# Gated linear attention feeding a cosine-gated MLP: token-major attention outputs turned on the tensor engine, and an order planned with new costs

## The chip, the cores and the metric

The kernel runs on one core of one Trainium2 chip. The metric is the device time of one execution in microseconds (us), as the median over several runs; lower is better. Names used below: PE is the tensor engine (PEld its weight loads), ACT the scalar engine, DVE the vector engine, POOL the GpSimd engine, SP the engine that only issues DMA here.

## The reference

Two stages follow each other. The first is a gated linear attention over 4 batches, 8 heads, 768 tokens and 48 channels; the second multiplies all 3072 tokens (384 features each) through an MLP with the gate h * cos(h):

```python
f = 1.0 / (1.0 + np.exp(-f_logit))
for t in range(S):
    state = f[:, :, t, :, None] * state + np.einsum('bhd,bhe->bhde', k[:, :, t], v[:, :, t])
    y[:, :, t] = np.einsum('bhd,bhde->bhe', q[:, :, t], state)
x = y.transpose(0, 2, 1, 3).reshape(B * S, H * D)      # 3072 x 384
h = x @ w_in                                           # 3072 x 2048
out = (h * np.cos(h)) @ w_out                          # 3072 x 384
```

## The kernel before

**Tiling.** The recurrence is cut into chunks of 128 tokens: 6 for each batch, 24 in all. Within a chunk the products of decays become a cumulative sum of logarithms, so that scaled q and k, one masked score matrix per head and one carried state per batch give the outputs by matmul. The MLP takes the finished chunks as units: four of 128 tokens, then ten of 256 (`UNITS`). Chunks go through the attention singly for the first four and in pairs after that (`GROUPS`).

**One chunk of attention**, with the lines of the listing:
- `chunk_load` (327) issues the DMAs of f, v, k and q, 192 KB each. Most go through SP. For chunk 0, k and q go through ACT; v of the first two chunks and q of the second go through POOL.
- `decay_group` (344) takes exp and log on ACT (352, 355), a cumulative sum on PE (367, 370), and two exponentials on ACT that give the scales b and bi (377).
- `attend` (385) scales q and k (395, 400, on POOL or DVE) and casts v to bf16 (404, POOL). The bf16 v goes into a buffer `vz` in which each head's 48 columns stand between zeros. Then q and k are turned so that channels lie on partitions: for chunks below `NPE` = 6 by twelve PE transposes and three evictions (421, 430, 432), for the others by one DMA transpose issued from SP (436). Scores are made by 8 matmuls (447) and masked on DVE (452). The new state takes 8 matmuls with 48 moving columns (466), then 475 and 479; it lies in `sz`, also between zeros.
- The outputs are made feature-major at once, which is the layout that the MLP reads as moving operand. For each of three blocks of 128 features, windows of `vz` (or `sz`) stand still and the masked scores (or turned q) move with 128 columns (506, 510). A window holds one head's columns at their place in the block and zeros around them. That gives 10 matmuls a chunk, and 6 more where there is a state. One copy (520 on ACT or 522 on DVE) brings the block to `xT`.

**One unit of the MLP** (`moe`, 526): groups of matmuls with w_in (540), each filling 512 columns of a PSUM bank; a Sin on ACT with a bias of pi/2 kept in a tile `halfpi` (547), which is the cosine; a product on DVE (551); then matmuls with w_out, 16 for each 128 tokens (561), a copy (570, 572) and the output DMA from SP (575).

**What sets the order.** Every operation is entered in a planner (`Plan`) with the engines that could run it and a cost in ns for each. `Plan.run` is a list scheduler: it takes the operation that could start first, gives it an engine and a buffer, and goes on. The kernel then issues exactly this order, so each engine runs a fixed list in sequence and waits on semaphores. A changed cost, buffer or dependence anywhere can therefore move instructions everywhere. Priorities only break ties. The weights come in eight DMAs from POOL (317), which the planner books on SP and which depend on chunk 0's v. PSUM has eight banks, shared by caps: scores 2, "mi" (sums, transposes, state, outputs) 4, MLP 5.

Of the kernel before, what the change touches and what calls it, by code (L numbers as in the profile page):

```python
# [9 lines left out]
F32 = mybir.dt.float32  # L10
BF16 = mybir.dt.bfloat16
AF = mybir.ActivationFunctionType
HALF_PI = math.pi / 2.0
# [78 lines left out]
class Op:  # L92
    __slots__ = ("seq", "eng", "fn", "prio", "table", "deps", "vals", "alloc", "start",
                 "end", "lat", "waiting", "after", "grp", "frees")


class Plan:


    SEM = 70.0  # L100

# [3 lines left out]
    def op(self, eng, fn, reads=(), writes=(), prio=0.0, table=None, lat=0.0, grp=None):  # L105
        o = Op()
        o.seq, o.fn, o.prio, o.table, o.lat, o.grp = len(self.ops), fn, prio, table, lat, grp
        o.eng, o.frees = eng, None
        o.deps, o.alloc, o.vals = set(), [], []
        for v in reads:  # L110
            o.deps.update(v.writers)
        for v in writes:
            w = getattr(v, "whole", v)
            if w.pool is not None:
                o.alloc.append(w)
            if v.writers:

                o.deps.add(v.writers[-1])
        for v in list(reads) + list(writes):
            v = getattr(v, "whole", v)  # L120
            if v.pool is not None and v not in o.vals:
                o.vals.append(v)
                v.uses += 1
        for v in writes:
            v.writers.append(o)
        o.after = []
        self.ops.append(o)
        return o
# [6 lines left out]
    def run(self):  # L135
        engs = ("PE", "ACT", "DVE", "POOL", "SP")
        free = dict.fromkeys(engs, 0.0)
        table, lock = "E", None
        left = {}
# [8 lines left out]
        n = len(self.ops)  # L148
        while len(order) < n:
            best = None  # L150
            for o in ready:
                at = max([d.end + (0.0 if e0 == d.eng == "PE" else self.SEM)
                          for d in o.deps for e0 in (next(iter(o.eng)),)], default=0.0)
                ok = True
                for v in o.alloc:
                    if v.slot is not None:
                        continue
                    b = v.pool.best()
                    if b is None:
                        ok = False  # L160
                        break
                    at = max(at, b[0] + self.SEM)
                if not ok:
                    continue
                pick = None
                for e, cost in o.eng.items():
                    if e == "ACT" and lock is not None and o.grp != lock and o.table is not None:
                        continue
                    s = max(at, free[e])
                    sw = 1300.0 if e == "ACT" and o.table not in (None, table) else 0.0  # L170
                    if pick is None or s + cost + sw < pick[0]:
                        pick = (s + cost + sw, s, e, cost)
                if pick is None:
                    continue
                key = (pick[1], o.prio, o.seq)
                if best is None or key < best[0]:
                    best = (key, pick[1], o, pick[2], pick[3])
# [16 lines left out]
            o.start, o.end = s, s + cost + o.lat  # L194
            free[e] = s + cost
            o.eng = e
# [20 lines left out]
def kernel(  # L217
# [23 lines left out]
    NPE = 6  # L241
# [31 lines left out]
    vS = slots("v", nld, [128, H, D], F32)  # L273
    spS = slots("sp", 5, [128, H, 64], zero=272.0)
# [3 lines left out]
    VW = D + 128  # L278
    vzS = slots("vz", 4, [128, H * VW + 128], zero=700.0)
    qktS = slots("qkt", 4, [128, 3 * NP, C])  # L280
    amS = slots("am", 4, [128, 4, C])
    SW = 128 + 2 * D + 128
    szS = slots("sz", 3, [128, NP, SW], zero=650.0)
# [26 lines left out]
    def load_weights(part, i, prio):  # L310
        if part == 0:
            dst = w_in_v[i]
            src = moe_w_in.rearrange("(km p) f -> p km f", p=128)[:, :, i * 512:(i + 1) * 512]
        else:
            dst = w_out_v[i]
            src = moe_w_out.rearrange("(kf p) m -> p kf m", p=128)[:, i * 4:(i + 1) * 4, :]
        o = P.op({"SP": 2000.0}, lambda e, dst=dst, src=src: nc.gpsimd.dma_start(
            out=dst.ap, in_=src), writes=[dst], prio=prio, lat=2500.0)
        o.deps.add(first_v[0])
# [5 lines left out]
    first_v = []  # L325

    def chunk_load(b, c, prio):
        vals = []
        for pool, src in ((fS, f_logit), (vS, v), (kS, k), (qS, q)):
            t = Val(pool)  # L330
            ap = src[b, :, c * C:(c + 1) * C, :].rearrange("h p d -> p h d")
            if prio < 1 and pool in (kS, qS):
                P.op({"ACT": 600.0}, lambda e, t=t, ap=ap: nc.scalar.dma_start(out=t.ap, in_=ap),
                     writes=[t], prio=prio, lat=3300.0)
            elif prio < 2 and pool in (vS, qS):
                o = P.op({"POOL": 1000.0}, lambda e, t=t, ap=ap: nc.gpsimd.dma_start(out=t.ap, in_=ap),
                         writes=[t], prio=prio, lat=3300.0)
            else:
                P.op({"SP": 1080.0}, lambda e, t=t, ap=ap: nc.sync.dma_start(out=t.ap, in_=ap),  # L339
                     writes=[t], prio=prio, lat=2200.0)  # L340
            vals.append(t)
        return vals
# [42 lines left out]
    def attend(b, c, ld, bt, bi, prio):  # L385
        _, vf, kf, qf = ld
        tok = b * S + c * C

        qk, vz = Val(qkS), Val(vzS)
# [9 lines left out]
        for par in range(2):  # L399
            P.op({"POOL": 550.0, "DVE": 350.0} if fast else {"POOL": 550.0}, lambda e, par=par: E(e).tensor_mul(  # L400
# [3 lines left out]
        o = P.op({"POOL": 510.0}, lambda e: nc.gpsimd.tensor_copy(  # L404
            out=vz.ap[:, 128:].rearrange("p (h w) -> p h w", w=VW)[:, :, 0:D], in_=vf.ap),
            reads=[vf], writes=[vz], prio=prio)
        first_v.append(o)
# [5 lines left out]
        if tok < NPE * C:  # L413
# [21 lines left out]
        else:  # L435
            P.op({"SP": 2000.0}, lambda e: nc.sync.dma_start_transpose(out=qkt.ap, in_=qk.ap),
                 reads=[qtd] + ktd, writes=[qdt] + kz, prio=prio, lat=2500.0)
# [22 lines left out]
        if c < NCH - 1:  # L460
            ps, S_out = Val(miS), Val(szS)

            def pes(e):
                o = ps.ap[:, 0:H * D].rearrange("p (h d) -> p h d", d=D)
                for h in range(H):
                    nc.tensor.matmul(o[:, h, :], lhsT=qk.ap[:, (NP + h) * C:(NP + h + 1) * C],  # L466
                                     rhs=vz.ap[:, 128 + h * VW:128 + h * VW + D],
                                     start=(h == 0), stop=(h == H - 1))
            P.op({"PE": 8 * 30.0}, pes, reads=ktd + [vz], writes=[ps], prio=prio, lat=170.0)
# [3 lines left out]
            else:  # L473
                st = Val(stS)
                P.op({"DVE": 530.0}, lambda e: nc.vector.tensor_add(  # L475
                    out=st.ap, in0=psv(), in1=S_in.ap[:, :, 128:128 + 2 * D]),
# [3 lines left out]
                out=S_out.ap[:, :, 128:128 + 2 * D], in0=srcap(),  # L480
# [5 lines left out]
        py = Val(miS)  # L486
        jobs = []
        for t in range(KM):
            for h in range(H):
                r = h * D - t * 128  # L490
                if -D < r < 128:
                    jobs.append((t, "a", h, r))
            if S_in is not None:
                for p in range(NP):
                    r = p * 2 * D - t * 128
                    if -2 * D < r < 128:
                        jobs.append((t, "s", p, r))

        def pey(e):
            o = py.ap.rearrange("p (a n) -> p a n", n=C)  # L500
            for i, (t, kind, n, r) in enumerate(jobs):
                first = all(j[0] != t for j in jobs[:i])
                fl = dict(start=(i == 0), stop=(i == len(jobs) - 1))
                if kind == "a":
                    w0 = 128 + n * VW - r
                    nc.tensor.matmul(o[:, t, :], lhsT=vz.ap[:, w0:w0 + 128],  # L506
                                     rhs=ams[n // 4].ap[:, n % 4, :], **fl)
                else:
                    w0 = 128 - r
                    nc.tensor.matmul(o[:, t, :], lhsT=S_in.ap[:, n, w0:w0 + 128],  # L510
                                     rhs=qdt.ap[:, n, :], **fl)
        rd = [vz, qdt] + ams + ([S_in] if S_in is not None else [])
        P.op({"PE": len(jobs) * N128}, pey, reads=rd, writes=[py], prio=prio, lat=170.0)
        x = xT[tok // C]

        def yev(e):
            d = x.ap
            s = py.ap[:, 0:KM * C].rearrange("p (a n) -> p a n", n=C)
            if e == "ACT":
                nc.scalar.copy(out=d, in_=s)  # L520
            else:
                nc.vector.tensor_copy(out=d, in_=s)
        P.op({"ACT": 380.0, "DVE": 530.0}, yev, reads=[py], writes=[x], prio=prio)


    def moe(t0, T):
# [6 lines left out]
        for j in range(KF // G):  # L533
            ph, co = Val(phS), Val(coS)

            def g1(e, j=j, ph=ph):
# [10 lines left out]
            P.op({"ACT": 640.0}, lambda e, ph=ph, co=co: nc.scalar.activation(  # L547
                out=co.ap, in_=ph.ap, func=AF.Sin, bias=halfpi),
# [6 lines left out]
        for i in range(T // 128):  # L555
# [12 lines left out]
            def ev(e, po=po, ot=ot):  # L568
# [7 lines left out]
                out=out[r0:r0 + 128, :], in_=ot.ap), reads=[ot], prio=pr, lat=2000.0)  # L576

    halfpi = cpool.tile([128, 1], F32, name="halfpi")
    nc.vector.memset(halfpi, HALF_PI)
# [59 lines left out]
```

## Time and profile before

| | before |
|---|---|
| median of 7 runs | 200.92 us (200.03 to 201.82) |
| the profiled execution: time, and span from first to last instruction | 201.82 us, 200.0 us |
| PE busy | 178.3 us, 1960 matmuls |
| ACT busy | 151.7 us |
| DVE busy | 143.0 us |
| POOL busy | 54.9 us |
| DMA | 34.15 MB, 171 GB/s over the span |

Busy time is the union of an engine's instructions. A matmul's row shows its latency, and matmuls overlap, so the pace of PE is read from the chain that ended last, where a run of n matmuls stands with the time it took. Idle time is put down to what released the engine. The granted PE clock is 1.00 over the whole core.

### The profile page before, as it was taken

What the parts mean: (1) busy time and instruction counts of PE and PEld (TensorE: products, weight loads), DVE (VectorE), ACT (ScalarE), POOL (GpSimd) and SP (SyncE); (2) the same over time, 40 slices, a digit from 0 to 9 for tenths busy, and PEclk for the clock granted to TensorE, in tenths of its full rate; (3) what the DMA queues carried; (4) which work ended last, traced back from release to release, by engine and by line L of the source; (5) the groups of instructions that cost most, each with busy time, mean ns of one, the idle gap of its engine ahead of it and who ended that gap; (6) DMA issues with size and microseconds to landing.
All of it is one profiled execution on the core that took longest, in us unless ns stands there. A gap on an engine that the chain in (4) does not pass through costs nothing.

```text
span 200.0 us, 5037 instructions
## 1 busy us (share of the span) xinstructions
PE 178.3 (89%) x1960; PEld 142.3 (71%) x1960; DVE 143.0 (71%) x248; ACT 151.7 (76%) x259; POOL 54.9 (27%) x86
## 2 busy tenths in 40 slices
PE   0359776989979999999999999999999999899992
PEld 0249765986868787787787887786887878678660
DVE  7865753775889889599689598598595998854500
ACT  4457746869999797798998799798796999727510
POOL 8775520412530230250301412711312316000000
PEclk9999999999999999999999999999999999999999
DMA  7999999999609989979999999898899855911012
GB/s 145 218 216 225 219 208 187 177 184 217 144 2 224 214 175 204 229 111 235 227 202 217 222 220 225 170 234 181 197 199 218 197 101 146 95 39 43 16 65 78
DMA packets 132328, 34.15 MB, mean 171 GB/s; under 512 B 125504, under 2 KB 132160, under 8 KB 132304
## 3 DMA queue, kind: packets, MB, share of 16 engines
q1 hardware_dynamic: 126320, 29.70, 72.5%
q0 software_dynamic: 3904, 3.74, 11.4%
q10 hardware_dynamic: 2080, 0.39, 1.0%
q8 instruction: 15, 0.25, 0.5%
q14 instruction: 9, 0.07, 0.1%
HBM read 25.17 MB, written 4.72 MB: 149 GB/s over the span
## 4 chain that ended last, share of the span: by engine, by line
PE 65%; DMA 15%; ACT 8%; issue 4%; DVE 3%; POOL 2%; SPq 2%; POOLq 0%; ACTq 0%; DVEq 0%
PE ps L561 25%; PE ps L540 24%; DMA qkt<-qk 7%; PE ps L506 5%; PE ps L447 5%; DMA w_out_bf<-in_moe_w_out_dram 4%; DMA v<-in_v_dram 4%; PE ps L510 2%; ACT b L377 2%; SPq L339 2%; PE ps L466 2%; PE ps L421 1%; ACT xT L520 1%; ACT bi L377 1%; ACT qkt L430 1%
## 5 line engine op out<-in xcount | busy, mean ns | idle before, releaser
L540 PE MATMUL ps<-xT,w_in_bf 128*128 128x256 bf16 (+1 forms) x672 | 70.1, 258 | 3.1 <-DMA w_in_bf<-in_moe_w_in_dram 1.6
L551 DVE TENSOR_TENSOR gT<-ps,cosh 128x512 bf16<-128x512 f32 x96 | 60.5, 683 | 15.4 <-ACT cosh L547 15.3
L561 PE MATMUL ps<-w_out_bf,gT 128*128 128x384 bf16 x384 | 70.1, 326 | 1.2 <-DMA w_out_bf<-in_moe_w_out_dram 1.1
L547 ACT ACTIVATE cosh<-ps,halfpi 128x512 bf16<-128x512 f32 x96 | 59.7, 694 | 8.3 <-PE ps L540 8.0
L540 PEld LDWEIGHTS <-w_in_bf 128*128 128x128 bf16 x672 | 57.4, 98 | 10.2 <-DMA w_in_bf<-in_moe_w_in_dram 1.8
L561 PEld LDWEIGHTS <-gT 128*128 128x128 bf16 x384 | 35.7, 98 | 20.7 <-issue 0.8
L452 DVE TENSOR_TENSOR am<-ps,umask 128x512 bf16<-128x512 f32 x48 | 30.9, 683 | 3.9 <-PE ps L447 3.2
L404 POOL CAST vz<-v 128x384 bf16<-128x384 f32 x24 | 12.8, 535 | 51.4 <-DMA v<-in_v_dram 30.2
L400 POOL TENSOR_TENSOR qk<-k,bi 128x192 bf16<-128x192 f32 x20 | 13.7, 686 | 36.0 <-ACT bi L377 27.0
L395 DVE TENSOR_TENSOR qk<-q,b 128x384 bf16<-128x384 f32 x21 | 12.6, 600 | 14.5 <-ACT b L377 14.5
L506 PE MATMUL ps<-am,vz 128*128 128x128 bf16 x240 | 22.3, 223 | 0.0
L479 POOL TENSOR_TENSOR sz<-st,b 128x384 bf16<-128x384 f32 x16 | 13.2, 825 | 27.0 <-DVE st L475 24.5
L570 ACT COPY ot<-ps 128x384 f32<-128x384 f32 x20 | 9.5, 475 | 14.2 <-PE ps L561 14.2
L447 PE MATMUL ps<-qkt 128*128 128x128 bf16 x192 | 16.3, 227 | 1.8 <-DMA qkt<-qk 1.2
L506 PEld LDWEIGHTS <-vz 128*128 128x128 bf16 x240 | 16.9, 100 | 1.4
L400 DVE TENSOR_TENSOR qk<-k,bi 128x192 bf16<-128x192 f32 x28 | 17.3, 631 | 0.0
L606 ACT ACT_TABLE_LOAD x12 | 15.4, 1283 | 2.2 <-issue 2.0
L510 PE MATMUL ps<-qkt,sz 128*128 128x128 bf16 x120 | 16.5, 219 | 0.0
L447 PEld LDWEIGHTS <-qkt 128*128 128x128 bf16 x192 | 12.9, 101 | 3.8 <-DMA qkt<-qk 2.0
L547 ACT ACT_TABLE_LOAD x12 | 15.4, 1283 | 0.2
L377 ACT ACTIVATE b<-ps 128x388 f32<-128x388 f32 x24 | 12.1, 503 | 3.7 <-PE ps L370 2.6
L367 PE MATMUL ps<-sp,umask 128*128 128x384 bf16 x24 | 8.0, 345 | 6.4 <-ACT sp L355 6.3
(38 smaller groups left out, 143.4 us busy)
## 6 DMA issues: line engine op xcount, KB each, us to landing
f<-in_f_logit_dram SPq DMA_DIRECT2D x24, 192.0 KB, 3.6
out_dram<-ot SPq DMA_DIRECT2D x24, 192.0 KB, 3.0
k<-in_k_dram SPq DMA_DIRECT2D x23, 192.0 KB, 4.2
v<-in_v_dram SPq DMA_DIRECT2D x22, 192.0 KB, 3.9
q<-in_q_dram SPq DMA_DIRECT2D x22, 192.0 KB, 3.8
w_in_bf<-in_moe_w_in_dram POOLq DMA_DIRECT2D x4, 384.0 KB, 5.8
w_out_bf<-in_moe_w_out_dram POOLq DMA_DIRECT2D x4, 384.0 KB, 7.8
v<-in_v_dram POOLq DMA_DIRECT2D x2, 192.0 KB, 6.2
```

The costliest lines, as they stand in the source:

```text
L377: nc.scalar.activation(out=o.ap, in_=pc.ap[:, 0:n], func=AF.Exp, scale=s)
L400: P.op({"POOL": 550.0, "DVE": 350.0} if fast else {"POOL": 550.0}, lambda e, par=par: E(e).tensor_mul(out=ktd[par].ap, in0=kf.ap[:, par:H: ...
L447: nc.tensor.matmul(o[:, i, :], lhsT=kz[g].ap[:, i, :], rhs=qdt.ap[:, h // 2, :], start=(i == 0), stop=(i == 3))
L452: nc.vector.tensor_mul(out=am.ap, in0=pa.ap.rearrange("p (a n) -> p a n", n=C), in1=umask[:, None, :].broadcast_to([128, 4, C]))
L479: P.op(cost, lambda e: E(e).tensor_mul(out=S_out.ap[:, :, 128:128 + 2 * D], in0=srcap(), in1=bt.ap[:, H * D:, None].broadcast_to([128, NP, ...
L506: nc.tensor.matmul(o[:, t, :], lhsT=vz.ap[:, w0:w0 + 128], rhs=ams[n // 4].ap[:, n % 4, :], **fl)
L510: nc.tensor.matmul(o[:, t, :], lhsT=S_in.ap[:, n, w0:w0 + 128], rhs=qdt.ap[:, n, :], **fl)
L540: nc.tensor.matmul(ph.ap[:, g * T:(g + 1) * T], lhsT=w_in_bf[:, m, f0:f0 + 128], rhs=x[:, m, :], start=(g == 0 and m == 0), stop=(g == G - ...
L547: P.op({"ACT": 640.0}, lambda e, ph=ph, co=co: nc.scalar.activation(out=co.ap, in_=ph.ap, func=AF.Sin, bias=halfpi), reads=[ph], writes=[c ...
L551: P.op({"DVE": 650.0}, lambda e, ph=ph, co=co, gv=gv: nc.vector.tensor_mul(out=gv.ap, in0=ph.ap.rearrange("p (g t) -> p g t", t=T), in1=co ...
L561: nc.tensor.matmul(po.ap[:, 0:d_model], lhsT=gT.ap[:, j, i * 128:(i + 1) * 128], rhs=w_out_bf[:, j, :], start=(j == 0), stop=(j == KF - 1))
L606: nc.scalar.preload_act_table_set("natural_log_exp_and_others")
```

## The change

Five things change.

1. The outputs of a chunk are made token-major. The masked scores of each head stand still, and v moves with 48 columns (8 matmuls); turned q stands still and the state of two heads moves with 96 columns (4 matmuls). So `vz` becomes a packed `vb`, `sz` loses its zeros, and their clearing goes. A copy brings the block to a bf16 tile `y`, three PE transposes turn it, and a second copy brings it to `xT`. (`NPX` is 24, so the branch that would turn it by DMA is never taken.)
2. `NPE` is 8 instead of 6: q and k are turned on PE for the first eight chunks, and by DMA from the ninth.
3. The Sin's bias is a constant in the instruction instead of the tile `halfpi`.
4. The weight DMAs are booked on POOL. Those of w_out depend on the k product of chunks 1 to 4 in turn, those of w_in on that of chunk 0. v and q of chunk 1 are loaded through SP, and chunk 0's k product is bound to POOL.
5. The planner gets a model of the two DMA rings and other costs for DMAs and for the Sin.

```diff
-    NPE = 6
+    GATES = [1, 2, 3, 4]
+    NPE, NPX, EVERY = 8, 24, 1
...
+                    if o.dma and e == "SP":
+                        s = max(s, ring[0] - self.RING)
...
-        o = P.op({"SP": 2000.0}, lambda e, dst=dst, src=src: nc.gpsimd.dma_start(
-            out=dst.ap, in_=src), writes=[dst], prio=prio, lat=2500.0)
-        o.deps.add(first_v[0])
+        o = P.op({"POOL": 850.0}, lambda e, dst=dst, src=src: nc.gpsimd.dma_start(
+            out=dst.ap, in_=src), writes=[dst], prio=prio, lat=2200.0, dma=2400.0 if part == 0 else 2200.0)
+        gate(o, 0 if part == 0 else GATES[i])
...
-            elif prio < 2 and pool in (vS, qS):
-                o = P.op({"POOL": 1000.0}, ...
+            elif prio < 1 and pool is vS:
+                eng, dma = {"POOL": 850.0}, nc.gpsimd
...
-            P.op({"POOL": 550.0, "DVE": 350.0} if fast else {"POOL": 550.0}, ...
+            o = P.op({"POOL": 550.0, "DVE": 350.0} if fast and tok else {"POOL": 550.0}, ...
...
-                    w0 = 128 + n * VW - r
-                    nc.tensor.matmul(o[:, t, :], lhsT=vz.ap[:, w0:w0 + 128],
-                                     rhs=ams[n // 4].ap[:, n % 4, :], **fl)
-                else:
-                    w0 = 128 - r
-                    nc.tensor.matmul(o[:, t, :], lhsT=S_in.ap[:, n, w0:w0 + 128],
-                                     rhs=qdt.ap[:, n, :], **fl)
+            for h in range(H):
+                nc.tensor.matmul(o[:, h, :], lhsT=ams[h // 4].ap[:, h % 4, :], rhs=vf.ap[:, h, :],
+                                 start=(h == 0), stop=(S_in is None and h == H - 1))
+            for p in range(NP if S_in is not None else 0):
+                nc.tensor.matmul(py.ap[:, p * 2 * D:(p + 1) * 2 * D], lhsT=qdt.ap[:, p, :],
+                                 rhs=S_in.ap[:, p, :], start=False, stop=(p == NP - 1))
...
-        P.op({"ACT": 380.0, "DVE": 530.0}, yev, reads=[py], writes=[x], prio=prio)
+        P.op({"ACT": 380.0, "DVE": 530.0}, copy(lambda: yt.ap, lambda: py.ap[:, 0:H * D]),
+             reads=[py], writes=[yt], prio=prio)
+                for t in range(KM):
+                    nc.tensor.transpose(out=pxv()[:, t, :], in_=yt.ap[:, t * C:(t + 1) * C],
+                                        identity=ident)
+            P.op({"PE": KM * N128}, tx, reads=[yt], writes=[px], prio=prio, lat=170.0)
+            P.op({"ACT": 380.0, "DVE": 330.0}, copy(lambda: x.ap, pxv), reads=[px], writes=[x],
+                 prio=prio)
...
-            P.op({"ACT": 640.0}, lambda e, ph=ph, co=co: nc.scalar.activation(
-                out=co.ap, in_=ph.ap, func=AF.Sin, bias=halfpi),
+            P.op({"ACT": 570.0}, lambda e, ph=ph, co=co: nc.scalar.activation(
+                out=co.ap, in_=ph.ap, func=AF.Sin, bias=HALF_PI),
```

## The prediction

> **What bounds the kernel now.** I read the page's busy times first, then four stretches of the span, then what PE waited for, then the chain of work that ended last for the pace of the matmuls, and the groups for durations.
>
> ```profile
> PE 178.3 (89%) x1960; PEld 142.3 (71%) x1960; DVE 143.0 (71%) x248; ACT 151.7 (76%) x259; POOL 54.9 (27%) x86
> ```
>
> PE leads, but 89% hides different stages. In the stretches the columns are length, then busy time of PE, PEld, DVE, ACT and POOL, the granted clock, the DMA share and GB/s:
>
> ```profile
> 0.00:18.30 18.30, 7.74 (x82) 6.73 (x83) 12.47 (x22) 9.32 (x18) 13.10 (x25) 1.00 1.12 199
> 18.30:60.00 41.70, 35.96 (x490) 29.91 (x489) 29.14 (x53) 32.89 (x53) 14.24 (x22) 1.00 0.93 169
> 60.00:170.00 110.00, 108.92 (x1183) 87.18 (x1181) 89.09 (x157) 96.36 (x168) 27.60 (x40) 1.00 0.94 198
> 170.00:200.00 30.00, 25.69 (x213) 18.46 (x210) 12.26 (x20) 13.12 (x23) 0.00 (x0) 1.00 0.26 56
> ```
>
> From 60 to 170 us PE is busy for 108.92 of 110 us, so there every microsecond taken off PE's list can come off the time. ACT (96.36, 88%) and DVE (81%) have some room, but not much. At the start PE waits: the first w_in matmul runs at 18.3 us. What PE waited for, in total, times, longest:
>
> ```profile
> PE ps L367 <- ACT sp L355: 6.3, 2, 5.4
> PE ps L421 <- POOL qk L395: 2.4, 1, 2.4
> PE ps L421 <- DVE qk L395: 2.0, 1, 2.0
> PE ps L540 <- DMA w_in_bf<-in_moe_w_in_dram: 1.6, 1, 1.6
> PE ps L447 <- DMA qkt<-qk: 1.2, 3, 0.5
> PE ps L561 <- DMA w_out_bf<-in_moe_w_out_dram: 1.1, 2, 0.6
> PE ps L540 <- ACT xT L520: 0.9, 2, 0.6
> ```
>
> The chain, as start, length and piece, gives the pace of each kind of matmul once they are back to back:
>
> ```profile
> 61.23 0.20 PE ps L466 x8
> 61.43 1.97 PE ps L540 x18
> 63.39 0.45 PE ps L447 x8
> 64.50 1.30 PE ps L561 x8
> 66.02 0.56 PE ps L506 x10
> ```
>
> That is 0.025 us for one with 48 moving columns, 0.056 with 128, 0.109 with 256, 0.163 with 384. Multiplied by the counts of the whole program (24 cumulative sums, 72 transposes, 192 scores, 160 state, 360 outputs, 192 + 480 with w_in, 384 with w_out) PE's list comes to 170.9 us. So some 29 us of the 200.0 us span are waiting: most of the first 18 us, 5.7 us up to 60 us, and about 4 us behind the last matmul.
>
> **Part by part: the outputs on PE.** Removed: 240 + 120 matmuls of lines 506 and 510 at 0.056 = 20.2 us. Added: 8 x 24 = 192 with 48 columns at 0.025 (the row of line 466, the same shape) = 4.8 us; 4 x 20 = 80 with 96 columns, which no row has: between 48 columns (0.025) and 128 (0.056) both ends give 2.0 and 4.5 us, and the line through 128 and 256 gives 0.043, so 3.4 us; 72 transposes at 0.056 (as line 447's 128 columns) = 4.0 us. Together 12.2, a saving of 7.9 us. Two more chunks with q and k turned on PE add 24 x 0.056 = 1.3 us. Net -6.6 us (164.3 us of PE work).
>
> Here a rule speaks against the change. The Trainium skill, "TensorE: Matmul & The Clock Gate", section "Back-to-back issue gap", says that in a stream of weight load and matmul pairs both set the spacing, about 81 ns at 128 columns. Each added matmul has its own 128-column weight load. If loads paced them at 0.081, the new outputs would cost (192 + 80 + 72) x 0.081 = 27.9 us against 360 x 0.081 = 29.2 before, and with the two chunks of transposes nothing would be left. The rows above decide: eight line-466 matmuls, each with its own load, took 0.20 us. I take the row, and keep the rule for the range.
>
> **The copies and ACT.** Counting the two built programs: ACT gets 16 y copies (0.479 each, the xT row) = +7.7, one xT copy less, 5 qkt copies less (0.586) = -2.9, 6 ot copies less = -2.9. DVE gets 8 y copies (0.557) = +4.5, 11 qkt (0.414) = +4.6, 6 ot (0.548) = +3.3, 10 k products less (0.631) = -6.3, a q product less = -0.6, six clearings less (3 x 0.698, 3 x 0.645) = -4.0, and xT copies that now read bf16: 12 at about 0.35 (estimate from qkt's 0.414 for 512) against 11 at 0.557 = -1.9. DVE: -0.6 us.
>
> The Sin loses its bias tile. The nearest row is the ACT copy of the same 128x512 size without one:
>
> ```profile
> L547 ACT ACTIVATE cosh<-ps,halfpi 128x512 bf16<-128x512 f32 x96 | 59.7, 694 | 8.3 <-PE ps L540 8.0
> L430 ACT COPY qkt<-ps 128x512 bf16<-128x512 bf16 x10 | 5.7, 591 | 6.7 <-PE ps L421 6.7
> ```
>
> The difference is 103 ns, but the operation and input type differ too. Bounds are nothing (all of it the operation) and 103 ns: 0 to -9.9 us. I take -9, near the row. ACT in sum: -7.6 us, or +1.4 if the bias is worth nothing. So neither ACT nor DVE gains load while PE sheds 6.6 us; POOL gets ten k products (0.686) and one q product (1.1), loses a clearing (1.4) and two loads' issue (1.9): +4.7 on 55 us, idle cover. Table loads stay 12 + 12.
>
> **The new wait.** Behind the outputs, a chunk now goes copy, PE, copy before the w_in matmuls can read it, where it was one copy. PE stands at the transposes until y is there: about 0.75 us behind the last output matmul (drain near 0.2, copy 0.48 to 0.56). In PE's new list, priced with the paces above, the work between the two is 0.7 to 1.8 us in 22 of 24 chunks; chunk 0 has 0.2 us, chunk 3 none. Queued behind the waiting transposes is the next w_out or w_in work. Cost: 0.75 for chunk 3, 0.5 for chunk 0, some hundredths for others: +1.5 us. Lower bound 0; upper bound under rivals. A further PSUM bank (px, within mi's four) can hold up sums; no PE wait on an eviction of mi stands in the list above beyond 0.7 us, so 0 to +2, taken +1 with other lateness of a new order.
>
> **The start.** Chunk 1's q product sat on POOL behind chunk 2's v cast, which waited for its load, and PE waited 2.4 us for it (line 395). In the new list it is on DVE right behind chunk 0's masks, about 1 us earlier; chunk 0's k product costs +0.6 us, both halves on POOL. The w_in issues of POOL stood at 9.2, 12.5, 14.9 and 18.7 us between waits; now the four stand together behind chunk 0's k product (about 10 to 13 us), so the 1.6 us wait for w_in should go. w_out pieces, at 20 to 36 us, now follow chunks 1 to 4: the 1.1 us goes too. Against it, DMA is full there (share 1.12), so what comes sooner pushes chunk 3's and 4's loads back; POOL's v cast of chunk 1 stands behind 3.2 us of issues; and w_out's DMAs wait for k products on POOL, with later v casts queued behind. Bounds -5 and +2; taken -2.5. SP issues as many DMAs as before (133), two of them loads instead of transposes.
>
> **The sum.** -6.6 (PE) + 1.5 (hop) + 1.0 (order) - 2.5 (start) = -6.6 us. The profiled execution took 201.82 us, span 200.0 and 1.8 around it, the slowest of the seven and 0.9 above the median; its span becomes 193.4. From the median: 200.9 - 6.6 = 194.3 us.
>
> **Rivals.**
>
> *DMA becomes the pace.* The DMA share is 0.94 from 60 to 170 us, at 198 GB/s, and POOL's v casts waited 30 us for loads. Two transposes less save 0.79 of 34.15 MB. Up to 170 us some 32.4 MB went, 191 GB/s; at that rate the loads end 4.1 us sooner, not 6.6 and more, and the start gives nothing: 197 us, and with part of the hop 198 to 200. Against it: slice 12 of the page moves only 2 GB/s, so the rings were not full all the time. Chance 0.18.
>
> *Slower: the hop is exposed.* Place: the three transposes per chunk, when the y copy is queued on ACT or DVE behind a Sin (0.69) or product that runs late. The gains (6.6 + 2.5) over 24 chunks are 0.38 us: from that mean exposure on the change loses. One Sin for each chunk is 16.6 us: 200.9 - 9.1 + 16.6 = 208 us; half of it is about no change. For it: ACT's list is dense (88%) and the copies' lists are fixed. Against it: ACT waited 8.0 us for line 510, so copies were ahead of PE, and PE waited for xT only 1.3 us. Chance 0.13 for slower, 202 to 208.
>
> *More gain.* The start gives its full 5 us and no hop shows: 190 us. Chance 0.04. That the change does not do what it says has little room: the counts are in the built program. Only the load-paced rule would void it, at about 200 us; it is within the 0.18.
>
> **How the numbers follow.** Forecast, 190.5 to 198: 0.65. A measurement of this kernel can tell about 0.5% (1.0 us) from no change. Faster by more: 0.65 + 0.04 + 0.14 of the DMA case = 0.83; within: 0.04; slower: 0.13. The range from 190.5 to 200.5 leaves out the slower case and the top gain.
>
> **What would show it.** Right: output matmuls of 48 columns at 0.025 and 96 near 0.043 in the chain; a Sin of 0.59 to 0.60; ACT's total near 144 and DVE's near 142 us; first w_in matmul near 16.5 us and no wait for w_in; PE busy about as full from 60 to 165 us; waits of PE for y copies about 1.5 us. Wrong: PE waits on y or xT copies above 9 us in sum, or PE idle behind loads or q/k DMA transposes in the middle, or a run of eight short matmuls above 0.4 us.

## The result, and the profile after

The changed kernel takes 198.59 us in the median of 13 runs (196.13 to 204.24); the kernel before takes 200.97 in 34 runs on the same chip. The ratio is 0.9831, with an interval of 0.9801 to 0.9861: 1.7% or 3.4 us faster, about half of the 6.6 us that were forecast. The ratio leaves out the executions that took over 1.5% more than the fastest of their kernel, none of the 34 before and 6 of the 13 after, the profiled one among them; the medians of all differ by 2.4 us.

The profiled execution took 199.56 us, with a span of 197.8. Its busy times on the page:

```profile
PE 175.8 (89%) x1968; PEld 137.1 (69%) x1968; DVE 141.4 (71%) x256; ACT 145.9 (74%) x263; POOL 58.7 (30%) x94
```

PE is busy for 2.5 us less, at the same 89%. ACT went down by 5.8 us and DVE by 1.6, POOL up by 3.8. The stretches, with the same columns as before (length, PE, PEld, DVE, ACT, POOL, clock, DMA share, GB/s):

```profile
0.00:18.30 18.30, 9.16 (x95) 7.60 (x96) 10.22 (x21) 8.89 (x17) 11.52 (x25) 1.00 1.10 182
18.30:60.00 41.70, 35.59 (x493) 28.79 (x492) 31.09 (x62) 31.61 (x53) 13.02 (x22) 0.96 1.07 192
60.00:170.00 110.00, 106.68 (x1201) 83.92 (x1199) 90.71 (x160) 94.97 (x176) 34.13 (x50) 1.00 0.94 188
170.00:198.00 28.00, 24.41 (x187) 16.75 (x185) 9.38 (x15) 10.41 (x20) 0.00 (x0) 1.00 0.13 50
```

PE's idle time, length less busy time, was 10.6, 5.7, 1.1 and 4.3 us in the four stretches; it is now 9.1, 6.1, 3.3 and about 3.4 (span less 170, less 24.4). The first stretch gained 1.4 us, the middle lost 2.2. And the second stretch has a clock of 0.96. In two pieces of it:

```profile
30.00:40.00 10.00, 6.82 (x73) 4.20 (x70) 7.10 (x14) 7.38 (x12) 3.05 (x5) 0.94 1.08 193
40.00:50.00 10.00, 8.79 (x119) 6.94 (x118) 6.63 (x14) 7.10 (x12) 4.36 (x8) 0.89 1.03 181
```

If the clock is either full or half, 0.94 and 0.89 mean 1.2 and 2.2 us at half clock, which stretches PE's work there by 1.7 us. What PE waited for (total, times, longest):

```profile
PE ps L391 <- ACT sp L379: 5.1, 1, 5.1
PE ps L583 <- DMA w_out_bf<-in_moe_w_out_dram: 3.2, 3, 1.4
PE ps L447 <- DVE qk L419: 2.1, 2, 1.6
PE ps L473 <- DMA qkt<-qk: 2.0, 1, 2.0
PE ps L447 <- POOL qk L424: 1.6, 2, 1.3
PE ps L538 <- DVE y L527: 1.0, 1, 1.0
...
PE ps L562 <- DMA w_in_bf<-in_moe_w_in_dram: 0.4, 1, 0.4
```

Line numbers have moved: L583 is w_out, L562 w_in, L447 the transposes of q and k, L473 the scores, L538 the new transposes of y. The wait for w_in is nearly gone (it was 1.6 us). The new hop, PE waiting for the copy of y before it can turn it, shows with 1.0 us, once. But w_out is now waited for 3.2 us, where it was 1.1, and one q/k DMA transpose for 2.0. The chain of work that ended last (start, length, piece) shows both, and the pace of the new matmuls:

```profile
32.22 6.55 DMA w_out_bf<-in_moe_w_out_dram
38.82 2.72 PE ps L583 x8
...
44.33 6.39 DMA w_out_bf<-in_moe_w_out_dram
...
53.53 0.20 PE ps L517 x8
53.73 0.17 PE ps L520 x4
...
54.82 0.17 PE ps L538 x3
...
93.39 7.67 DMA qkt<-qk
```

Eight output matmuls with 48 columns take 0.20 us, four with 96 take 0.17 (0.043 each), three transposes 0.17: the prices of the forecast. Eight w_out matmuls took 1.30 us before and 2.72 at 38.82 us: that is half clock. Two short waits stand right before them, one for y and one for this weight (in brackets the idle time before, and what ended it):

```profile
37.06 0.34 PE L538 MATMUL ps<-ident,y 128*128 128x128 bf16 x3 [1.02 <-DVE y L527]
38.82 2.72 PE L583 MATMUL ps<-w_out_bf,gT 128*128 128x384 bf16 x8 [1.42 <-DMA w_out_bf<-in_moe_w_out_dram]
```

The timeline shows why the weight came so late. First SP's own issues (start, length), then POOL's list:

```profile
12.50 6.93 SPq L363 DMA_DIRECT2D k<-in_k_dram  x1
19.48 5.47 SPq L363 DMA_DIRECT2D q<-in_q_dram  x1
```
```profile
28.96 0.50 POOL L429 CAST vb<-v 128x384 bf16<-128x384 f32 x1 [6.64 <-DMA v<-in_v_dram]
...
32.22 0.81 POOL L336 DMA_DIRECT2D w_out_bf<-in_moe_w_out_dram  x1
```

While the four w_in DMAs and the first w_out DMAs are under way, SP needs 6.93 and 5.47 us to issue two loads of chunk 3. In this execution the v of the same chunk, issued at 11.47, lets POOL's cast start only at 28.96. POOL waits 6.64 us for it, and behind it in POOL's list stands the third w_out issue.

Last, the Sin without its bias tile, as a group (total, mean ns, idle before):

```profile
L569 ACT ACTIVATE cosh<-ps 128x512 bf16<-128x512 f32 x96 | 53.4, 604 | 8.1 <-PE ps L562 4.8 <-DVE am L478 1.1
```

### The profile page after: what moved, and what is told of

The parts are those of the page before. It is cut to its first block, busy times and chain, and to the rows that moved or that the text cites. A ratio compares the mean times of both kernels' runs of the same rounds, so it can differ in the third digit from the quotient of the medians.

```text
span 197.8 us, 5063 instructions
## 1 busy us (share of the span) xinstructions
PE 175.8 (89%) x1968; PEld 137.1 (69%) x1968; DVE 141.4 (71%) x256; ACT 145.9 (74%) x263; POOL 58.7 (30%) x94
## 4 chain that ended last, share of the span: by engine, by line
PE 56%; DMA 21%; SPq 7%; POOL 6%; DVE 4%; issue 3%; ACT 1%; POOLq 0%; DVEq 0%; ACTq 0%
PE ps L583 24%; PE ps L562 22%; DMA w_out_bf<-in_moe_w_out_dram 13%; DMA qkt<-qk 4%; SPq L363 4%; SPq L462 3%; PE ps L473 3%; DMA q<-in_q_dram 2%; DMA v<-in_v_dram 2%; DVE am L478 2%; POOL w_in_bf L336 2%; POOL qk L424 1%; PE ps L391 1%; PE ps L517 1%; PE ps L520 1%
## 5 line engine op out<-in xcount | busy, mean ns | idle before, releaser
L583 PE MATMUL ps<-w_out_bf,gT 128*128 128x384 bf16 x384 | 72.4, 330 | 3.4 <-DMA w_out_bf<-in_moe_w_out_dram 3.2
L562 PE MATMUL ps<-xT,w_in_bf 128*128 128x256 bf16 (+1 forms) x672 | 70.3, 260 | 0.8 <-DMA w_in_bf<-in_moe_w_in_dram 0.4
L562 PEld LDWEIGHTS <-w_in_bf 128*128 128x128 bf16 x672 | 58.3, 99 | 8.3 <-issue 1.1
L569 ACT ACTIVATE cosh<-ps 128x512 bf16<-128x512 f32 x96 | 53.4, 604 | 8.1 <-PE ps L562 4.8
L583 PEld LDWEIGHTS <-gT 128*128 128x128 bf16 x384 | 35.6, 98 | 22.8 <-issue 4.3
L424 POOL TENSOR_TENSOR qk<-k,bi 128x192 bf16<-128x192 f32 x30 | 19.6, 664 | 23.3 <-ACT bi L401 14.9
L429 POOL CAST vb<-v 128x384 bf16<-128x384 f32 x24 | 12.9, 539 | 35.9 <-DMA v<-in_v_dram 21.7
L419 DVE TENSOR_TENSOR qk<-q,b 128x384 bf16<-128x384 f32 x20 | 13.1, 653 | 13.8 <-ACT b L401 10.6
L473 PE MATMUL ps<-qkt 128*128 128x128 bf16 x192 | 16.7, 227 | 2.1 <-DMA qkt<-qk 2.0
L592 ACT COPY ot<-ps 128x384 f32<-128x384 f32 x14 | 6.7, 479 | 13.3 <-PE ps L583 13.3
L473 PEld LDWEIGHTS <-qkt 128*128 128x128 bf16 x192 | 12.5, 101 | 3.4 <-DMA qkt<-qk 2.3
L527 ACT CAST y<-ps 128x384 bf16<-128x384 f32 x16 | 7.7, 480 | 8.4 <-PE ps L517 4.5
L447 PE MATMUL ps<-ident,qk 128*128 128x128 bf16 x96 | 9.7, 242 | 4.2 <-DVE qk L419 2.1
L376 ACT ACTIVATE f<-f 128x384 f32<-128x384 f32 x24 | 11.6, 517 | 1.1 <-DMA f<-in_f_logit_dram 1.0
L401 ACT ACTIVATE bi<-ps 128x384 f32<-128x384 f32 x24 | 12.0, 500 | 0.0
```

Of the source, the lines that this page charges most:

```text
L401: nc.scalar.activation(out=o.ap, in_=pc.ap[:, 0:n], func=AF.Exp, scale=s)
L419: P.op({"POOL": 1000.0, "DVE": 560.0} if fast else {"POOL": 1000.0}, lambda e: E(e).tensor_mul(out=qtd.ap, in0=qf.ap, in1=bt.ap[:, 0:H * D ...
L424: o = P.op({"POOL": 550.0, "DVE": 350.0} if fast and tok else {"POOL": 550.0}, lambda e, par=par: E(e).tensor_mul(out=ktd[par].ap, in0=kf. ...
L429: P.op({"POOL": 510.0}, lambda e: nc.gpsimd.tensor_copy(out=vf.ap, in_=v32.ap), reads=[v32], writes=[vf], prio=prio)
L473: nc.tensor.matmul(o[:, i, :], lhsT=kz[g].ap[:, i, :], rhs=qdt.ap[:, h // 2, :], start=(i == 0), stop=(i == 3))
L562: nc.tensor.matmul(ph.ap[:, g * T:(g + 1) * T], lhsT=w_in_bf[:, m, f0:f0 + 128], rhs=x[:, m, :], start=(g == 0 and m == 0), stop=(g == G - ...
```

## Experiments

The change bundles the outputs, the bias and a new plan. The theory was that the outputs on PE make the gain, and that the plan's start and the DMA queues take some of it back. The rivals: the bias or the plan alone make it, or the copies on ACT and DVE take the rest. A ratio is always to the kernel before on the same chip, with its 95% interval.

**e1: the bias alone.** The kernel before, all lists as they were:

```diff
-                out=co.ap, in_=ph.ap, func=AF.Sin, bias=halfpi),
+                out=co.ap, in_=ph.ap, func=AF.Sin, bias=HALF_PI),
```

> The kernel before with one edit: the Sin takes pi/2 as a constant instead of the tile halfpi; the planned cost stays, so every engine's list is unchanged. Theory (PE sets the time, ACT has room): Sin rows of about 0.60 instead of 0.69 us, ACT busy about 143 us, time 200 to 201 us, no more than 0.7 us better. Rival (the lighter Sin is what made the changed kernel faster): about 198 us.

0.9997 (0.9969 to 1.0025). The group in the profile of this run:

```profile
L547 ACT ACTIVATE cosh<-ps 128x512 bf16<-128x512 f32 x96 | 53.5, 601 | 13.4 <-PE ps L540 11.5
```

The Sin is 93 ns shorter (694 before), ACT has 6.2 us less work, and its idle time before the Sin grew from 8.3 to 13.4 us. Nothing is gained: ACT waited for PE.

**e2: the outputs alone.** Part 1 of the change in the kernel before, planned anew; bias tile, `NPE` = 6, DMA order and costs as before:

```diff
-                    nc.tensor.matmul(o[:, t, :], lhsT=vz.ap[:, w0:w0 + 128],
-                                     rhs=ams[n // 4].ap[:, n % 4, :], **fl)
+                nc.tensor.matmul(o[:, h, :], lhsT=ams[h // 4].ap[:, h % 4, :], rhs=vf.ap[:, h, :],
```

> The kernel before with the token-major outputs alone: packed v, 8 + 4 short matmuls, y copy, three PE transposes, second copy; NPE 6, the Sin's tile and the old planner and DMA costs stay. Theory (PE's saving is real and PE sets the time): PE's list falls by 20.2 - 12.2 = 7.9 us, some of it returned at the hop; 194 to 197 us. Rival (the copies and the hop eat it, and the gain of the changed kernel comes from the new planning and the Sin): 200 us or more.

1.0003 (0.9973 to 1.0032): nothing gained, and my expectation failed. Two stretches:

```profile
18.30:60.00 41.70, 32.69 (x456) 25.91 (x453) 29.38 (x55) 29.15 (x49) 12.13 (x19) 1.00 1.00 177
60.00:170.00 110.00, 106.10 (x1178) 82.68 (x1179) 94.28 (x164) 99.75 (x173) 29.94 (x44) 1.00 0.97 195
```

PE's busy time fell by 6.0 us (172.3), and its idle time rose from 21.7 to 27.5: 3.3 us more between 18 and 60 us (9.0 against 5.7) and 2.8 more in the middle (3.9 against 1.1). The saving is real, and this order can't use it.

**e3: third and fourth w_out early.** The changed kernel, with these two DMAs moved to directly behind the second in POOL's list; no other list changes:

```diff
+    for o in w_out_ops[2:]:
+        order.remove(o)
+    i = order.index(w_out_ops[1]) + 1
+    order[i:i] = w_out_ops[2:]
```

> The changed kernel with the third and fourth w_out DMA issued right behind the second in POOL's list, which is the only list that differs. Theory (late w_out pieces made PE wait 3.2 us and slowed its clock near 37 to 50 us): no PE wait for w_out beyond 0.6 us, granted clock 1.00 in 30 to 50 us, 194.5 to 196.5 us. Rival (the DMA rings are full in the first 50 us, so the wait only moves): PE waits as long for the loads of chunks 3 and 4, 198 to 199 us.

0.9895 (0.9833 to 0.9958); the interval overlaps that of the changed kernel, so it is no better, and perhaps worse. The first wait of PE, the stretch it lies in, and two issues near its start:

```profile
PE ps L450 <- DVE qk L422: 9.4, 3, 7.1
```
```profile
20.00:30.00 10.00, 4.95 (x52) 4.95 (x53) 3.95 (x8) 1.43 (x3) 2.62 (x4) 0.53 1.26 185
```
```profile
9.04 3.10 POOL L336 DMA_DIRECT2D w_in_bf<-in_moe_w_in_dram  x4
10.24 0.68 SPq L366 DMA_DIRECT2D q<-in_q_dram  x1
```

The w_out wait is gone from the list. In its place PE waits up to 7.1 us for the scaled q of chunk 2, because DVE waits as long for its load; and the clock is 0.53. That looks like the rival, but this wait does not need the edit: the load was issued at 10.24 us, and the moved DMAs only behind 19.51. In e11, where w_out is issued as in the changed kernel, PE waits longer for the same q:

```profile
PE ps L447 <- DVE qk L419: 10.2, 3, 8.4
```

What these two traces share is the order of the first issues: this load went out 1.2 us behind the first w_in DMA, and DVE could use it at 24.4 us here and at 26.3 us in e11. In the traces of the changed kernel and of e4 it went out 0.2 us ahead of that DMA and together with it (9.48 and 9.70 against 9.67), and DVE used it at 17.9 and 19.5 us. So about 1 us of difference among the first DMAs goes with 5 to 8 us at this load; this is a reading across traces, and no run tests it. Whether early w_out pushes other loads back stays open. The middle is fuller here than in the changed kernel's profile (PE 108.29 of 110 us), so the late transpose there does not belong to every execution.

**e4: more PE work.** The changed kernel with the y transposes issued twice, 72 x 0.056 = 4.0 us of PE work, lists as they were:

```diff
-                for t in range(KM):
+                for t in list(range(KM)) * 2:
```

> The changed kernel with the three y transposes of each chunk issued twice, the second time over the first; all lists keep their order. PE gets 72 x 0.056 = 4.0 us more. Theory (PE sets the time): 198.6 + 4 = about 202.5 us. Rival (PE has slack since the change, something else sets the time): 198.6 to 200 us.

0.9958 (0.9925 to 0.9991), 1.3% or 2.6 us above the changed kernel: between the two theories. A microsecond of PE work is worth about 0.6 us (0.4 to 0.9 from the two intervals).

The trace of this run has the changed kernel's order and a clock of 1.00 throughout. Two stretches, then two waits and the w_out matmuls that ran at half clock above:

```profile
18.30:60.00 41.70, 37.62 (x543) 31.32 (x542) 33.54 (x67) 34.64 (x59) 13.12 (x22) 1.00 1.08 196
60.00:170.00 110.00, 105.74 (x1210) 83.30 (x1209) 87.23 (x155) 91.29 (x168) 32.85 (x49) 1.00 0.94 186
```
```profile
PE ps L473 <- DMA qkt<-qk: 2.8, 3, 1.4
...
PE ps L583 <- DMA w_out_bf<-in_moe_w_out_dram: 0.6, 2, 0.3
```
```profile
38.14 1.46 PE L583 MATMUL ps<-w_out_bf,gT 128*128 128x384 bf16 x8 [0.32 <-DMA w_out_bf<-in_moe_w_out_dram]
```

PE's idle time is 9.1 us in the first stretch, then 4.1 and 4.3. The third w_out DMA is issued as late as in the changed kernel's profile (32.47 against 32.22 us), but it lands sooner, PE waits 0.32 us, and the clock holds. So the long w_out waits and the half clock do not belong to every execution of this order. Here the idle time stands in the middle, and 2.8 us of it are waits for q/k DMA transposes.

**e5, e6, e7: less to load.** From the seventh chunk on each load brings heads 0 to 3 only, in the kernel before (e5), in e2 (e6) and in the changed kernel (e7), lists as they were:

```diff
+            n = 4 if prio >= 6 else 8
-            P.op(eng, lambda e, t=t, ap=ap, dma=dma: dma.dma_start(out=t.ap, in_=ap),
+            P.op(eng, lambda e, t=t, ap=ap, dma=dma, n=n: dma.dma_start(
+                out=t.ap[:, 0:n, :], in_=ap[:, 0:n, :]),
```

> The kernel before, in which the loads of f, v, k and q from the seventh chunk on bring heads 0 to 3 only (the other half of each tile keeps older data); every list keeps its order. Theory now (full DMA rings hold PE up, and that is where the outputs' saving went): little to gain here, since PE waits only 1.1 us from 60 to 170 us, though the weights of the start land sooner; 199 to 200.5 us. Rival (DMA holds nothing up): no change, 201 us.

> The kernel before with the token-major outputs alone (as in e2), and with the same half loads from the seventh chunk on. Theory (the rings ate the 7.9 us that PE sheds): with the rings free the saving shows, 194 to 196 us. Rival (ACT and DVE ate it: 99.8 and 94.3 us busy of 110, the copies and the heavy Sin): no change against e2, 200 us or more.

> The changed kernel with the same half loads from the seventh chunk on. Theory (w_out and the loads of chunks 3 and 4 land late behind a full ring, and a pair of q/k DMA transposes in the middle): PE's waits for w_out and for transposes go, 193.5 to 195.5 us. Rival (the order on ACT and DVE is what holds PE): 197.5 to 198.6 us.

e5 gives 1.0024 (0.9994 to 1.0055), e6 1.0020 (0.9984 to 1.0056), e7 0.9715 (0.9686 to 0.9743). The middle of e6, and then of e7:

```profile
60.00:170.00 110.00, 106.61 (x1182) 83.22 (x1180) 94.21 (x163) 100.15 (x173) 30.69 (x44) 1.00 0.66 143
```
```profile
60.00:170.00 110.00, 108.72 (x1226) 86.01 (x1224) 92.82 (x164) 97.14 (x178) 33.71 (x49) 1.00 0.62 133
```

In e6 a DMA share of 0.66 instead of 0.97 moves neither the time nor PE's 106 us: the queues did not eat the saving of e2. The changed kernel gains 1.2% (2.3 us); PE waits for no q/k transpose from 60 us on, and the slowest of them lands 4.9 us after its issue instead of 7.7. (PE's 108.72 us in the middle prove less: e11, with whole loads and a later start, has 108.72 too.) So transfers cost nothing in the kernel before and 2.3 us in the changed one, which is the forecast's rival "DMA becomes the pace", in part. With the loads halved in both kernels, e7 against e5, the change is worth 3.1% or 6.2 us (0.9715 / 1.0024).

**e8: everything but the outputs.** The changed kernel with its other four parts, but outputs feature-major from `vz` and `sz`, planned anew:

```diff
-                nc.tensor.matmul(o[:, h, :], lhsT=ams[h // 4].ap[:, h % 4, :], rhs=vf.ap[:, h, :],
+                    nc.tensor.matmul(o[:, t, :], lhsT=vz.ap[:, w0:w0 + 128],
+                                     rhs=ams[n // 4].ap[:, n % 4, :], **fl)
```

> The changed kernel with the outputs feature-major again (padded v and state, 10 or 16 matmuls of 128 columns, one copy); planner, DMA model, gates, NPE 8 and the Sin's constant stay. PE's list grows by 7.9 us, ACT and DVE lose the y copies. Theory (the outputs pay once ACT is lighter and the DMAs are planned): 202 to 205 us, so that the outputs are worth 4 to 6 us in this surrounding. Rival (the planning and the Sin made the gain, the outputs nothing, as e2 suggests): 198 to 199.5 us.

1.0041 (1.0013 to 1.0069). Its middle:

```profile
60.00:170.00 110.00, 108.78 (x1193) 87.51 (x1191) 89.20 (x152) 89.08 (x164) 32.87 (x47) 1.00 0.93 184
```

PE is full here, and no time is gained: constant bias, new plan and `NPE` 8 are worth nothing without the outputs. With them the kernel is 2.1% faster (1.0041 / 0.9831), 4.2 us. So the same outputs bring nothing in the old plan (e2) and 4.2 us in the new. Both comparisons are between two plans, so what a plan is worth by itself (e10) lies inside both figures.

**e9: outputs and bias.** e2 with the constant bias, lists as in e2 (the edit is that of e1).

> The kernel before with the token-major outputs (as in e2) and the Sin's bias as a constant; the planned cost of the Sin stays 640, so every engine's list is that of e2. Theory now (in e2 ACT and DVE, with the y copies on top, hold PE up in each decay stage, and the lighter Sin pays for them): ACT busy falls by 8 to 9 us, and 197 to 199.5 us. Rival (the order of the lists holds PE up, however short the rows are): as e2, 201.5 to 202 us.

0.9973 (0.9941 to 1.0005), its interval overlapping that of e2. Its middle:

```profile
60.00:170.00 110.00, 105.89 (x1180) 82.51 (x1177) 94.34 (x164) 95.69 (x173) 29.43 (x42) 1.00 0.96 194
```

ACT is relieved by 4.1 us there and PE is as before (105.89; e2 106.10). So ACT's load is not what e2's idle time came from.

**e10: the same, planned for it.** e9 with the planner told the Sin's real length, so that it plans anew; DMA planning and `NPE` of the kernel before:

```diff
-            P.op({"ACT": 640.0}, lambda e, ph=ph, co=co: nc.scalar.activation(
+            P.op({"ACT": 570.0}, lambda e, ph=ph, co=co: nc.scalar.activation(
```

> As e9, but the planner is told 570 for the Sin, so the lists are made anew; NPE 6, DMA planning, gates and loads stay as in the kernel before. Theory (outputs and lighter Sin together make the gain, each nothing alone): 196 to 198.5 us, as good as the changed kernel. Rival (the new DMA planning and NPE 8 are needed as well): 200 us or more.

1.0172 (1.0128 to 1.0215), 2% slower than e9 with the same instructions in another order. Two stretches and one wait:

```profile
20.00:30.00 10.00, 6.91 (x78) 6.60 (x76) 4.32 (x8) 2.58 (x5) 0.94 (x2) 0.66 1.22 190
```
```profile
60.00:170.00 110.00, 104.48 (x1158) 80.60 (x1157) 94.08 (x167) 95.32 (x171) 28.61 (x41) 1.00 0.96 193
```
```profile
PE ps L531 <- DMA w_in_bf<-in_moe_w_in_dram: 2.8, 2, 2.6
```

PE idles 5.5 us in the middle alone. And part of the 2% is clock: it is 0.66 from 20 to 30 us, where the long w_in wait lies, and PE is busy for 176.2 us in all against 173.5 in e9's trace. The outputs need the rest of the new planning, as the rival said, or luck with the order.

**e11: the bias tile back.** The changed kernel with `bias=halfpi` (the edit of e1, reversed), lists as they were.

> The changed kernel with the Sin's bias in the tile halfpi again; the planned cost stays 570, so the lists stay, apart from the tile's own clearing at the start of DVE. ACT gets 96 x 0.09 = 8.6 us more. Theory (the outputs pay only with the lighter Sin): the gain is lost, 200 to 203 us. Rival (ACT has room, and the Sin is idle cover as in e1): 198 to 199 us.

0.9891 (0.9819 to 0.9963). It overlaps the changed kernel's interval; at the centre it is 0.6% or 1.2 us, and the two intervals together allow anything from nothing to 2.8 us. ACT is busy for 5.8 us more (151.7 against 145.9): the rival, that ACT has room, is the nearer one.

**e12: NPE 6.** The changed kernel, planned anew with one number changed:

```diff
-    NPE, NPX, EVERY = 8, 24, 1
+    NPE, NPX, EVERY = 6, 24, 1
```

> The changed kernel with NPE 6: chunks 7 and 8 have their q and k turned by DMA again, and the lists are made anew. PE loses 24 x 0.056 = 1.3 us and ACT and DVE six evictions; the rings get two transposes (0.79 MB) while the late w_out pieces and loads are on their way. Theory (full rings are what is left of PE's waits, as the half loads' 2.3 us show): 199 to 201 us, so NPE 8 is worth 1 to 2 us. Rival (PE's 1.3 us count for more): 197 to 198 us.

1.0125 (1.0065 to 1.0185), 3% slower than the changed kernel, although PE has 1.3 us less to do. A wait and a stretch:

```profile
PE ps L447 <- DVE qk L419: 8.5, 3, 6.7
```
```profile
20.00:30.00 10.00, 4.83 (x63) 4.83 (x64) 4.13 (x9) 1.78 (x3) 1.20 (x2) 0.66 1.17 185
```

PE again waits long for chunk 2's q while the weights come, and the clock is 0.66. This is the wait that e11 shows with `NPE` 8, so it is not what `NPE` 6 costs. More is lost than either theory gave; the whole plan moved with the number, so this does not price DMA transposes, and where the 3% come from stays open.

## Why the prediction was right, and its gain twice too large

**The outputs on PE (-7.9, with the added turns -6.6): the work was sized right.** The chain's paces are those of the sum. (PE's 170.9 us hold 2.4 us for the 96 short matmuls of line 370, which the forecast's list of counts leaves out.) The rule weighed against it, the Trainium skill, "TensorE: Matmul & The Clock Gate", section "Back-to-back issue gap", has 81 ns at 128 columns, where the chain has 56. Carried over to eight output matmuls it would make 0.65 us, an estimate from that page; they took 0.20. But the step from work to time failed. "Every microsecond taken off PE's list can come off the time" was read from 108.92 of 110 us. The runs give 0 in the old plan (e2), 4.2 us of 7.9 in the new (e8 against the changed kernel), and about 0.6 for each microsecond added (e4). What PE then waits for is in part known: in the new plan transfers (e7); in the old one neither transfers (e6) nor ACT's load (e9), and that cause stays open. PE's busy row fell by only 2.5 us: 1.7 us of the difference is half clock, and the other 2.4 I can't place.

**The Sin and the copies: right, and without weight.** 604 ns against 0.59 to 0.60 us, ACT 145.9 against 144 us, DVE 141.4 against 142. At the centre, the runs with and without the constant (e1, e9, e11) differ by 0 to 1.2 us.

**The hop (+1.5): right.** One wait of 1.0 us for y; the slower rival, an exposed hop in each chunk, is out.

**The start (-2.5): right in one trace, wrong in others.** In the profile of the changed kernel the first half came: the first w_in matmul at 16.99 us (16.5 forecast, 18.29 before), w_in waits 0.4. The second, "the 1.1 us goes too" for w_out, did not: 3.2 us of waits and 1.7 us of half clock, which the sum did not have at all. The forecast had named the cause as a risk (w_out behind k products, v casts in POOL's list) and gave it no price. From the start to 60 us PE's idle time went from 16.3 to 15.2 us, and the clock took more than that back. In e4's trace, with the same order and the clock at 1.00, it went to 13.2 us, near the forecast, although the added transposes fill some of it; in e11's it is 21.4. So the start is a spread, not one number.

**The order (+1.0) and the middle "about as full": the failed term.** PE idles 3.3 us there instead of 1.1, and 4.3 in e4's trace; 2.0 and 2.8 us of that stand behind q/k DMA transposes, which the forecast had listed as a sign of being wrong. It is the rival "DMA becomes the pace", which had a chance of 0.18 and nothing in the sum. The reason given against it, a slice with 2 GB/s, does not bear on the middle: that slice is the twelfth, at 55 to 60 us. e7 prices the transfers at 2.3 us. Four traces with nearly the same order agree with it, though none is a test of it: PE's idle time up to 60 us is 13.2, 15.2, 18.0 and 21.4 us (e4, changed, e3, e11), and in the middle 4.3, 3.3, 1.7 and 1.3. In them, the earlier the start, the more PE waits later, so that a gain at the start is not kept whole.

Together: with halved loads the change is worth 6.2 us, close to the sum's 6.6, and with whole loads the 3.4 us measured. The 198.59 us lie just above the forecast's own band (190.5 to 198) and in that of the DMA rival (197, or 198 to 200 with part of the hop). The whole range, up to 200.5, had room for almost any gain, so that it held is in part luck. This leaves open which part of the new planning (gates of the weights, costs of DMAs, `NPE`) lets the outputs pay; e10 and e12 each change the whole order. No variant with all of the work beat the changed kernel.

## What to carry to other kernels

Saved work of the busiest engine is not saved time where the order is fixed beforehand: add a known piece of work to that engine, and take some off the loads, and see what each costs or brings, before a saving is multiplied out. Compare an edit with the lists held as they are, for a new plan alone is worth as much as most edits (2% between e9 and e10, the clock included). At the start, price a burst of weight DMAs by the loads it delays and by the clock that the matrix engine loses while it waits, not by its bytes.

## What the runs showed of the hardware

- One 192 KB load took SP 6.93 us to issue while the weight DMAs from POOL were under way; a few microseconds later, at 29 to 33 us, the same issue took 0.7 to 0.9.
- At one place of the order, eight w_out matmuls took 1.46 us behind a wait of 0.32 us for their weight (e4), and 2.32, 2.72 and 2.10 us behind waits of 1.12, 1.42 and 2.02 us (e7, the changed kernel, e11), each with a wait of 1.02 or 1.03 us for y just before. In the changed kernel the half clock lasted some 3.4 us. In e3, with a wait of 7.1 us, the mean over 20 to 30 us is 0.53.
- The constant bias in place of a tile saves 90 ns on each Sin (694 to 604); the Trainium skill, "ScalarE: Activation LUTs", section "What ACT_TABLE_LOAD costs", states about 93 for a pointer operand.
